# Attention, two mixture layers, one core: loads ahead of the constants, summed exponentials per block, later w_in conversion, rows in fixed tiles

## The chip, the cores and the metric

One NeuronCore of a Trainium2 chip runs the whole program. The metric is the device time of one execution in microseconds (us), as the median of several runs. One further execution is recorded by the hardware profiler; its span and its rows are what the profile shows.

Engines: PE (TensorE, matmuls; its weight loads are listed as PEld), DVE (VectorE), ACT (ScalarE), POOL (GpSimd), SP (SyncE, which issues nearly all DMAs here; SPq is its queue). TensorE's clock has two levels, 1.2 and 2.4 GHz; the profile gives the granted clock as a share of the higher one.

## What is computed

```python
# attention: batch 4, heads 8, sequence 576, head size 64
scores = q @ k.T / 8
# heads 0 to 3 ("local"):   key within the 32 positions up to the query
# heads 4 to 7 ("strided"): key not after the query, same position modulo 32
attn = softmax(where(mask, scores, -1e9)) @ v
x = attn.transpose(0, 2, 1, 3).reshape(2304, 512)
# layer 1, d_ff 2048
x2 = (s * relu(x @ w_in) ** 2 + b) @ w_out
# layer 2: 8 experts, 288 tokens each, assigned greedily by sorted gate logits
logits = x2 @ w_gate
for e in range(8):
    out[assigned == e] = relu(x2[assigned == e] @ w1[e]) @ w2[e]
```

w_in and w_out arrive as 64-bit floats, as pairs of 32-bit words, and are converted on the chip.

## The kernel before

The program is written out in Python in the order in which each engine shall run it (`manual_schedule`): every engine works through its own list in order and waits only for semaphores. A `Pipe` holds generators; each `tick` runs each live generator to its next `yield`, and after every so many ticks starts a new one. So the place of an instruction in its engine's list follows from the number of ticks between the yields.

- **Attention** (`attn_unit`): one unit is a batch, a pair of heads and a half of the sequence; a batch has 8 units, in the order strided, strided, local (5 blocks of 96 columns), strided, strided, local (5 blocks), local (4 blocks), local (4 blocks). A unit loads qk and v (L194 to L206; qk has 4 buffers), puts mask and scores into one PSUM bank (L225, L232), takes the maximum per block on DVE (L237), subtracts it (L244), takes Exp on ACT (L247), sums (L249), inverts and scales on DVE (L250 to L252), transposes on PE (L258, L260), copies the transposes on ACT (L268), multiplies by v (L279) and copies into xb (L284, L288). A unit starts every 2 ticks; I number units from 1.
- **keep_warm** (L296): matmuls on constants, between units, in ticks 5 to 17.
- **prep**: one block of w_in or w_out (fc, 16 of each). Two loads `raw` (L325), Abs on ACT (L350), the conversion on DVE (L353 to L359), then for w_in a split into wh (ACT, L333) and wl (DVE, L335), so that a product is made of wh x xh + wh x xl + wl x xh.
- **group_x** splits 384 tokens of x the same way, for each of 4 feature blocks dc: xh (ACT, L315), xl (DVE, L316).
- **Main loop** (`mix1`): step n is `h_step(g, fc)` with 12 matmuls (L427) for token group g and block fc, then Relu and Square on ACT and a store of the result to `ud`. The first 24 steps alternate between groups 0 and 1. Beside the steps run the rest of w_in, batches 2 and 3 of attention, then w_out (`prep1`), and from step 46 the folds.
- **fold_late** reloads a stored block r from `ud`, three ticks to a step, and **fold_step** multiplies four of them by wog (L464): the gate logits.
- **late_step / x2_late**: the second product (L640) on reloaded r, split into u (ACT L610, DVE L613); **x2_row** (L481) scales the sum of 128 tokens into a row tile on DVE and stores it in x2d. These matmuls also fill `route`, which assigns tokens to experts on DVE. Then come the experts (L894, L919).

The tiles of the pool `w` (68 buffers of 128x512) hold nearly everything: raw, K, W, wh, wl, r, local E, eT, v and before the change the rows of x2_row. Strided units use three fixed tiles, E0 to E2 (`self.Es`).

Of the kernel before, what the change touches and what calls it, by code (L numbers as in the profile page):

```python
# [8 lines left out]
F32 = mybir.dt.float32  # L9
F32R = mybir.dt.float32r  # L10
BF = mybir.dt.bfloat16
# [51 lines left out]
class Body:  # L63
# [27 lines left out]
    P0S = 20  # L91
# [16 lines left out]
    KS = 5  # L108
    KE = 18
# [26 lines left out]
    def constants(self):  # L136
        nc, c, a = self.nc, self.c, self.a
        ts = nc.vector.tensor_scalar
# [3 lines left out]
        self.identf = c.tile([128, 128], F32, name="identf")  # L142
        ts(self.identf, jp[:, :128], 0.0, None, op0=ALU.is_equal)
        self.identb = c.tile([128, 128], BF, name="identb")
        ts(self.identb, jp[:, :128], 0.0, None, op0=ALU.is_equal)
        self.onesf = c.tile([128, 128], F32, name="onesf")
        nc.gpsimd.memset(self.onesf, 1.0)

        t1 = self.wt([128, 512], F32, "t1")
        t2 = self.wt([128, 512], F32, "t2")  # L150
        tt = nc.vector.tensor_tensor
        ts(jp[64:, :128], jp[64:, :128], 64.0, None, op0=ALU.add)
        self.Es = [c.tile([128, 8, 64], F32, name=f"E{i}") for i in range(self.NE)]
        for E in self.Es:
            nc.gpsimd.memset(E, 0.0)
        self.mstr = c.tile([128, 8, 36], BF, name="mstr")
        nc.vector.memset(self.mstr, 0.0)
        j4 = self.wt([128, 512], I32, "j4")
        nc.gpsimd.iota(j4[:, :36], pattern=[[1, 36]], base=0, channel_multiplier=0)
        nc.gpsimd.iota(j4[:, 64:100], pattern=[[0, 36]], base=0, channel_multiplier=1)  # L160
        for o in (0, 64):
            ts(j4[:, 128 + o:164 + o], j4[:, o:o + 36], 1, None, op0=ALU.bitwise_and)
# [6 lines left out]

# [8 lines left out]
        self.sb = c.tile([128, 2], F32, name="sb")  # L178
        for i, n in enumerate(("s", "b")):
            src = a[n]  # L180
            nc.sync.dma_start(self.sb[:, i:i + 1],
                              bass.AP(tensor=src.tensor, offset=src.offset, ap=[[0, 128], [1, 1]]))

# [30 lines left out]
    def attn_unit(self, b, hp, hf):  # L214
# [25 lines left out]
        else:  # L240
# [3 lines left out]
        nc.vector.tensor_tensor(E[:pr], sp[:pr, :w].rearrange("p (c k) -> p c k", c=nb),  # L244
                                mx.unsqueeze(2).to_broadcast([pr, nb, kw]), op=ALU.add)
        yield from self.lag(0, b)
        nc.scalar.activation(E[:pr], E[:pr], AF.Exp, scale=0.125)  # L247
        yield from self.lag(1, b)
        nc.vector.tensor_reduce(sm, E[:pr], axis=AX.X, op=ALU.add)  # L249
# [54 lines left out]
    def group_x(self, g, dc):  # L304
# [13 lines left out]
        self.xg.setdefault(g, []).append((h, l))  # L318
# [71 lines left out]
    def prep_begin(self):  # L390
# [5 lines left out]
        self.nc.vector.memset(self.wog, 0.0)  # L396
        self.gate = self.c.tile([128, 4, 8], F32, name="gate")
        self.nc.sync.dma_start(self.gate, self.a["gate"].rearrange("(c p) e -> p c e", p=128))
# [45 lines left out]
    def fold_late(self, g, fc):  # L444
# [3 lines left out]
        yield  # L448
        self.fold_step(fc, g, r)
# [27 lines left out]
    def x2_row(self, g, t, acc):  # L477
        nc = self.nc
        row = self.wt([128, 512], F32, "x2")
        i = g * 3 + t  # L480
        nc.vector.scalar_tensor_tensor(row, acc[t], self.sb[:, 0:1], self.acc, op0=ALU.mult, op1=ALU.add)  # L481
# [32 lines left out]
    def mix1(self):  # L514
        nc = self.nc
        self.L = self.c.tile([128, 18, 8], F32, name="L")
# [3 lines left out]
        nc.gpsimd.iota(self.R, pattern=[[0, 18], [1, 8]], base=1, channel_multiplier=0,  # L520
                       allow_small_or_imprecise_dtypes=True)
        self.x2d = self.dr.tile([self.N, self.DM], F32, name="x2d")
        self.ud = {g: self.dr.tile([16, 128, self.G], F32, name=f"ud{g}") for g in range(6)}
        self.prep_begin()
        self.pf, self.xacc = {}, {}
        att, att2 = (Pipe(self.attention(*b), self.AE) for b in ((0, 1), (2, 3)))
# [7 lines left out]
        z = self.wt([128, 512], F32, "z")  # L534
        nc.gpsimd.memset(z, 0.0)
        nc.sync.dma_start(self.x2d[self.N - 128:, :], z)
# [7 lines left out]
        k = 0  # L544
        while self.units < 14 or not self.win:
            att.tick()
            if self.KS <= k < self.KE:
                self.keep_warm(self.KW)
# [542 lines left out]
```

## Time and profile before

| | |
|---|---|
| time, median of 3 runs | 850.44 us (848.18 to 854.85) |
| the profiled execution | 850.04 us |
| its span, from first to last instruction | 848.3 us |
| PE busy | 808.2 us (95%) |
| DVE busy | 481.2 us (57%) |
| ACT busy | 363.4 us (43%) |
| chain that ended last, by engine | PE 87%, DVE 6%, DMA 3% |
| granted clock of PE, mean | 0.98 |

Shares over the whole span hide the stages: an engine that is busy for 57% of the whole may be the only one that matters in one stretch. So the tables by stretch and the chain of waits, which follows the work back from the end, come first, and groups of instructions give the prices.

### The profile page before, as it was taken

To read this page: it belongs to the slowest core of one execution; us is meant where nothing else is said; L and a number is where in the kernel's file an instruction comes from. 1 tells how busy PE (TensorE), PEld (TensorE's weight loads), DVE (VectorE), ACT (ScalarE), POOL (GpSimd) and SP (SyncE) were. 2 spreads that over 40 slices of the span, in tenths; PEclk is the share of its full clock that TensorE was granted. 3 is DMA by queue.
4 is the path that set the end of the run, shared out by engine and by line. 5 is a ranking of instruction groups with operands and counts; after the bars stand their busy time and mean duration, and the time that the engine had idled before them with its cause. 6 is when DMAs were issued, how large, how long until landed. Compare 5 with 4: busy or idle time off the path is not lost.

```text
span 848.3 us, 17237 instructions
## 1 busy us (share of the span) xinstructions
PE 808.2 (95%) x6688; PEld 702.7 (83%) x6688; DVE 481.2 (57%) x1166; ACT 363.4 (43%) x824; POOL 52.4 (6%) x70
## 2 busy tenths in 40 slices
PE   6968999999899999989999998998999999999996
PEld 4748998989789867967777776767899999999994
DVE  7899873576455033255777666647255555565530
ACT  1558665556345456432222222222055545554520
POOL 1000000000000000000000000000111112121211
PEclk9978999999999999999999999998999999999999
DMA  7764744765676597360706142324185576657400
GB/s 199 233 228 127 241 146 129 234 217 174 219 234 211 183 314 254 105 222 5 244 13 228 58 129 73 97 90 125 59 284 172 168 232 204 173 181 216 134 29 28
DMA packets 88754, 140.22 MB, mean 165 GB/s; under 512 B 10848, under 2 KB 52576, under 8 KB 88672
## 3 DMA queue, kind: packets, MB, share of 16 engines
q1 hardware_dynamic: 85600, 129.68, 48.4%
q0 software_dynamic: 3072, 9.44, 3.4%
q8 instruction: 52, 0.85, 0.4%
q14 instruction: 30, 0.25, 0.1%
HBM read 106.32 MB, written 32.77 MB: 164 GB/s over the span
## 4 chain that ended last, share of the span: by engine, by line
PE 87%; DVE 6%; DMA 3%; issue 1%; ACT 1%; SPq 0%; POOL 0%; POOLq 0%; DVEq 0%
PE b L427 24%; PE b L640 21%; PE b L894 12%; PE b L919 11%; PE b L232 3%; PE b L464 2%; PE b L769 2%; PE b L279 2%; PE b L957 1%; PE b L848 1%; PE b L382 1%; DMA r<-ud 1%; PE b L935 1%; PE b L296 1%; DMA x2d<-x 1%
## 5 line engine op out<-in xcount | busy, mean ns | idle before, releaser
L640 PE MATMUL b<-wh,u 128*128 128x512 f32 x544 | 185.6, 411 | 7.3 <-DVE u L613 7.3
L640 PEld LDWEIGHTS b<-wh,u 128*128 128x128 f32 x544 | 103.7, 193 | 30.0 <-DVE u L613 9.5
L610 ACT CAST u<-r 128x384 fp32r<-128x384 f32 (+1 forms) x96 | 47.3, 496 | 170.9 <-PE b L640 114.1
L640 PE MATMUL b<-wl,u 128*128 128x512 f32 x272 | 108.2, 398 | 0.0
L432 ACT ACTIVATE r<-b 128x384 f32<-128x384 f32 x96 | 47.1, 491 | 111.0 <-PE b L427 110.7
L919 PE MATMUL b<-u,wh 128*128 128x288 f32 x448 | 93.4, 301 | 0.0
L427 PE MATMUL b<-xh,wh 128*128 128x384 f32 x384 | 90.6, 358 | 2.7 <-ACT xh L315 2.7
L427 PE MATMUL b<-xl,wh 128*128 128x384 f32 x384 | 83.7, 339 | 0.0
L335 DVE TENSOR_TENSOR wl<-raw,wh 128x512 fp32r<-128x512 f32 x128 | 82.8, 683 | 1.4 <-DMA x2d<-x 1.1
L427 PE MATMUL b<-xh,wl 128*128 128x384 f32 x384 | 82.7, 336 | 0.0
L894 PE MATMUL b<-X,wh 128*128 128x288 f32 x512 | 78.2, 295 | 0.6 <-ACT X L867 0.6
L427 PEld LDWEIGHTS b<-xh,wh 128*128 128x128 f32 x384 | 65.2, 191 | 16.3 <-issue 9.1
L333 ACT CAST wh<-raw 128x512 fp32r<-128x512 f32 x128 | 73.5, 620 | 4.0 <-DVE u L613 4.0
L894 PEld LDWEIGHTS b<-X,wh 128*128 128x128 f32 x512 | 71.6, 188 | 1.4 <-ACT X L867 0.7
L919 PEld LDWEIGHTS b<-u,wh 128*128 128x128 f32 x448 | 70.9, 188 | 0.0
L427 PEld LDWEIGHTS b<-xl,wh 128*128 128x128 f32 x384 | 69.5, 190 | 0.4 <-DVE xl L316 0.4
L427 PEld LDWEIGHTS b<-xh,wl 128*128 128x128 f32 x384 | 68.7, 190 | 0.0
L901 DVE SCALAR_TENSOR_TENSOR u<-b,u 128x288 fp32r<-128x288 f32 x64 | 29.1, 454 | 66.4 <-ACT u L900 57.7
L919 PE MATMUL b<-u,wl 128*128 128x288 f32 x224 | 65.8, 294 | 0.0
L613 DVE TENSOR_TENSOR u<-r,u 128x384 fp32r<-128x384 f32 (+1 forms) x96 | 48.9, 529 | 23.3 <-ACT u L610 23.3
L640 PEld LDWEIGHTS b<-wl,u 128*128 128x128 f32 x272 | 52.4, 193 | 9.7
L900 ACT ACTIVATE u<-b 128x288 fp32r<-128x288 f32 x64 | 26.3, 412 | 59.2 <-PE b L894 57.2
(196 smaller groups left out, 1158.6 us busy)
## 6 DMA issues: line engine op xcount, KB each, us to landing
raw<-in_moe_w_dram SPq DMA_DIRECT2D x128, 256.0 KB
r<-ud SPq DMA_DIRECT2D x160, 192.0 KB
ud<-r SPq DMA_DIRECT2D x96, 192.0 KB
raw<-in_words_dram SPq DMA_DIRECT2D x64, 256.0 KB
qk<-in_q_dram SPq DMA_DIRECT2D x24, 288.0 KB
x2d<-x SPq DMA_DIRECT2D x18, 256.0 KB
wod<-K SPq DMA_DIRECT2D x16, 256.0 KB
wo<-wod SPq DMA_DIRECT2D x16, 256.0 KB
```

The source lines that it names most:

```text
L232: nc.tensor.matmul(sp[64 * j:64 * j + p, c * kw:(c + 1) * kw], qk[sl, 0, q0:q0 + p], qk[sl, 1, k0:k0 + kw], start=False, stop=(c == nb - 1 ...
L333: nc.scalar.copy(h, W)
L335: nc.vector.tensor_tensor(l, W, _f(h), op=ALU.subtract)
L427: nc.tensor.matmul(ps[:, :self.G], w[:, dc * 128:(dc + 1) * 128], self.xg[g][dc][x], start=(k == 0), stop=(k == 11))
L432: nc.scalar.activation(r, ps[:, :self.G], AF.Relu)
L610: nc.scalar.copy(d[:, 0, :], src)
L613: nc.vector.tensor_tensor(d[:, 1, :], src, _f(d[:, 0, :]), op=ALU.subtract)
L640: self.nc.tensor.matmul(**args)
L894: self.nc.tensor.matmul(ps[:, :288], w1[dc, fh][wi][:, fs:fs + 128], X[:, xi, dc, :], start=(k == 0), stop=(k == 11))
L900: self.nc.scalar.activation(h, ps[:, :288], AF.Relu)
L901: self.nc.vector.scalar_tensor_tensor(l, ps[:, :288], 0.0, _f(h), op0=ALU.max, op1=ALU.subtract)
L919: nc.tensor.matmul(y[dc][:, :288], w[:, sl], u[:, j, :288], start=(fc == 0 and i == 0), stop=(fc == 7 and i == 2))
```

## The change

- The first two ticks of attention, with the loads of the first units, stand ahead of `constants`, and the constants are in another order, with a one-element Exp at their head. sb, gate and the store of zeros to x2d move to tick 12 (`small_loads`); the zeros are now filled by DVE instead of POOL, and wog and R move there too.
- For local units of batches 0 and 1, the subtraction on DVE, the one Exp over all blocks and the sum on DVE become one Exp for each block on ACT, straight from PSUM, with the negated and scaled maximum as its bias and the sum as its second output. The maximum is scaled on DVE.
- The conversion of w_in starts at tick 24 instead of 20; the splits of x for groups 0 and 1 are made as soon as their units are done, inside the loop, instead of behind it.
- `fold_late` has a third yield. `x2_row` writes into E0 to E2 in turn.

```diff
-    P0S = 20
+    P0S = 24
+    SL = 12
+    SEG = 2
...
     def constants(self):
         nc, c, a = self.nc, self.c, self.a
-        ts = nc.vector.tensor_scalar
+        ts, tt = nc.vector.tensor_scalar, nc.vector.tensor_tensor
+        warm = c.tile([128, 1], F32, name="warm")
+        nc.vector.memset(warm, 0.0)
+        nc.scalar.activation(warm, warm, AF.Exp)
...
+    def small_loads(self):
+        nc, a = self.nc, self.a
         for i, n in enumerate(("s", "b")):
             src = a[n]
             nc.sync.dma_start(self.sb[:, i:i + 1],
                               bass.AP(tensor=src.tensor, offset=src.offset, ap=[[0, 128], [1, 1]]))
+        nc.sync.dma_start(self.gate, a["gate"].rearrange("(c p) e -> p c e", p=128))
+        z = self.wt([128, 512], F32, "z")
+        nc.vector.memset(z, 0.0)
+        nc.sync.dma_start(self.x2d[self.N - 128:, :], z)
...
-        nc.vector.tensor_tensor(E[:pr], sp[:pr, :w].rearrange("p (c k) -> p c k", c=nb),
-                                mx.unsqueeze(2).to_broadcast([pr, nb, kw]), op=ALU.add)
-        yield from self.lag(0, b)
-        nc.scalar.activation(E[:pr], E[:pr], AF.Exp, scale=0.125)
-        yield from self.lag(1, b)
-        nc.vector.tensor_reduce(sm, E[:pr], axis=AX.X, op=ALU.add)
+        if loc and b < self.SEG:
+            nc.vector.tensor_scalar(mx, mx, 0.125, None, op0=ALU.mult)
+            yield from self.lag(0, b)
+            for c in range(nb):
+                nc.scalar.activation(E[:pr, c, :], sp[:pr, c * kw:(c + 1) * kw], AF.Exp, bias=mx[:, c:c + 1],
+                                     scale=0.125, accum_out=sm[:, c:c + 1])
+            yield from self.lag(1, b)
+        else:
+            nc.vector.tensor_tensor(E[:pr], sp[:pr, :w].rearrange("p (c k) -> p c k", c=nb),
+                                    mx.unsqueeze(2).to_broadcast([pr, nb, kw]), op=ALU.add)
+            yield from self.lag(0, b)
+            nc.scalar.activation(E[:pr], E[:pr], AF.Exp, scale=0.125)
+            yield from self.lag(1, b)
+            nc.vector.tensor_reduce(sm, E[:pr], axis=AX.X, op=ALU.add)
...
-        self.xg.setdefault(g, []).append((h, l))
+        self.xg.setdefault(g, {})[dc] = h, l
...
-        self.nc.vector.memset(self.wog, 0.0)
         self.gate = self.c.tile([128, 4, 8], F32, name="gate")
-        self.nc.sync.dma_start(self.gate, self.a["gate"].rearrange("(c p) e -> p c e", p=128))
+        self.sb = self.c.tile([128, 2], F32, name="sb")
...
     def fold_late(self, g, fc):
         r = self.wt([128, self.G], F32, "r")
         self.nc.sync.dma_start(r, self.ud[g][fc])
+        yield
         yield
         yield
         self.fold_step(fc, g, r)
...
     def x2_row(self, g, t, acc):
         nc = self.nc
-        row = self.wt([128, 512], F32, "x2")
         i = g * 3 + t
+        row = self.Es[i % self.NE].rearrange("p c k -> p (c k)")
         nc.vector.scalar_tensor_tensor(row, acc[t], self.sb[:, 0:1], self.acc, op0=ALU.mult, op1=ALU.add)
         nc.sync.dma_start(self.x2d[i * 128:(i + 1) * 128, :], row)
         return row
...
+        self.prep_begin()
+        att, att2 = (Pipe(self.attention(*b), self.AE) for b in ((0, 1), (2, 3)))
+        att.tick(self.AE)
+        self.constants()
         self.L = self.c.tile([128, 18, 8], F32, name="L")
         self.R = self.c.tile([128, 18, 8], F32, name="R")
         self.ge = self.c.tile([128, 18, 8], F32, name="ge")
         self.ranked = set()
...
-        nc.gpsimd.iota(self.R, pattern=[[0, 18], [1, 8]], base=1, channel_multiplier=0,
-                       allow_small_or_imprecise_dtypes=True)
...
-        self.prep_begin()
         self.pf, self.xacc = {}, {}
-        att, att2 = (Pipe(self.attention(*b), self.AE) for b in ((0, 1), (2, 3)))
...
-        z = self.wt([128, 512], F32, "z")
-        nc.gpsimd.memset(z, 0.0)
-        nc.sync.dma_start(self.x2d[self.N - 128:, :], z)
...
-        k = 0
-        while self.units < 14 or not self.win:
+        ready = [(8, 0, dc) for dc in range(4)] + [(10, 1, 2), (11, 1, 0), (13, 1, 3), (14, 1, 1)]
+        k = self.AE
+        while self.units < 14 or not self.win or ready:
             att.tick()
+            if k == self.SL:
+                self.small_loads()
+                nc.vector.memset(self.wog, 0.0)
+                nc.gpsimd.iota(self.R, pattern=[[0, 18], [1, 8]], base=1, channel_multiplier=0,
+                               allow_small_or_imprecise_dtypes=True)
+            while ready and self.units >= ready[0][0]:
+                self.group_x(*ready.pop(0)[1:])
             if self.KS <= k < self.KE:
                 self.keep_warm(self.KW)
             if k >= self.P0S and k % self.P0R == 0:
                 prep.tick()
             k += 1
-        for g in range(2):
-            for dc in range(4):
-                self.group_x(g, dc)
+        assert not ready
...
     def run(self):
         import contextlib
         with self.tc.manual_schedule() if self.MANUAL else contextlib.nullcontext():
-            self.constants()
             self.mix1()
```

On SyncE's queue, at the start of the program (qk and v are attention's loads, sb, gate and z the small ones), before:

```order
L181 DMA sb<-in_moe_s_dram 128x1
L181 DMA sb<-in_moe_b_dram 128x1
L398 DMA gate<-in_gate_dram 128x4x8
L536 DMA x2d<-z_138 128x512
L194 DMA qk_141<-in_q_dram 128x2x288
L199 DMA v_143<-in_vs_dram 36x512 x2
```

The same place after the change:

```order
L201 DMA qk_82<-in_q_dram 128x2x288
L206 DMA v_84<-in_vs_dram 36x512 x2
L201 DMA qk_159<-in_q_dram 128x2x288
L206 DMA v_161<-in_vs_dram 36x512 x2
L201 DMA qk_186<-in_q_dram 128x2x320
L209 DMA v_188<-in_v_dram 96x512
```

The four small DMAs are gone from the head of the queue; they stand behind the loads of unit 7.

On DVE, from the maximum of unit 15 (a local unit of 4 blocks) on; unit 14 is the local unit before it, K and W are a block of w_in in conversion, nm holds maximum and sum, before:

```order
L237 TENSOR_REDUCE nm_925<-b_890 128x4
L244 TENSOR_TENSOR E_927<-b_890,nm_925 128x384
L249 TENSOR_REDUCE nm_859<-E_861 128x5
L250 TENSOR_SCALAR nm_859<-nm_859 128x5
L251 RECIPROCAL nm_859<-nm_859 128x5
L252 TENSOR_TENSOR E_861<-E_861,nm_859 128x480
L353 TENSOR_SCALAR K_911<-K_911 128x512
L354 TENSOR_SCALAR K_911<-K_911 128x512
L356 SCALAR_TENSOR_TENSOR W_960<-raw_679,K_911 128x256
L356 SCALAR_TENSOR_TENSOR W_960<-raw_681,K_911 128x256
L359 SCALAR_TENSOR_TENSOR K_911<-raw_679,W_960 128x256
L359 SCALAR_TENSOR_TENSOR K_911<-raw_681,W_960 128x256
```

The same place after the change:

```order
L244 TENSOR_REDUCE nm_940<-b_915 128x4
L252 TENSOR_SCALAR nm_940<-nm_940 128x4
L331 TENSOR_TENSOR xl_945<-xb_388,xh_944 128x192
L331 TENSOR_TENSOR xl_945<-xb_870,xh_944 128x192
L265 TENSOR_SCALAR nm_880<-nm_880 128x5
L266 RECIPROCAL nm_880<-nm_880 128x5
L267 TENSOR_TENSOR E_882<-E_882,nm_880 128x480
L244 TENSOR_REDUCE nm_993<-b_970 128x4
L252 TENSOR_SCALAR nm_993<-nm_993 128x4
L331 TENSOR_TENSOR xl_998<-xb_388,xh_997 128x192
```

The subtraction and the sum of the local units are gone, the second block's conversion stands behind unit 16's maximum now, and splits of x stand where conversions stood.

On PE, at the first fold (four matmuls on reloaded r, L464, L479 after the change; L427 and L441 are steps of the main loop, L279 and L294 attention's last product), before:

```order
L427 MATMUL b_3205<-xh_2416,wl_2008 128x384
L382 MATMUL b_3222<-gate,WT_3177 128x8 x4
L375 MATMUL b_3227<-identf,K_3038 128x128 x4
L464 MATMUL b_3152<-r_3148,wog 32x384
L464 MATMUL b_3152<-r_3150,wog 32x384
L464 MATMUL b_3152<-r_3153,wog 32x384
L464 MATMUL b_3152<-r_3246,wog 32x384
L427 MATMUL b_3260<-xh_3068,wh_957 128x384
```

The same place after the change:

```order
L441 MATMUL b_3279<-xh_3240,wl_1079 128x384
L294 MATMUL b_3302<-eT_3264,v_2774 64x64 x2
L294 MATMUL b_3302<-eT_3266,v_2774 64x64 x2
L294 MATMUL b_3302<-eT_3264,v_2774 64x64 x2
L294 MATMUL b_3302<-eT_3266,v_2774 64x64 x2
L479 MATMUL b_3268<-r_3171,wog 32x384
L479 MATMUL b_3268<-r_3173,wog 32x384
L479 MATMUL b_3268<-r_3175,wog 32x384
L479 MATMUL b_3268<-r_3269,wog 32x384
L441 MATMUL b_3324<-xh_3091,wh_1125 128x384
```

The fold stands behind the 49th step instead of the 48th; the second one moves from behind the 52nd to behind the 54th.

## Rows read from the trace of the kernel before

**Rows 1.** Chain of waits, 0 to 120 us: start, length, what

```profile
5.89 4.38 DMA qk<-in_q_dram
...
37.01 0.67 DVE nm L237
...
46.91 0.35 DVE K L353
...
49.17 0.48 DVE nm L237
...
63.94 0.02 ACT wh L333
...
66.00 6.67 PE b L427 x24
...
73.28 16.84 PE b L427 x96
```

**Rows 2.** Busy time by stretch: stretch, PE, PEld, DVE, ACT, POOL, PEclk, DMA share, GB/s

```profile
36.00:66.00 30.00, 19.21 (x395) 15.05 (x395) 28.46 (x74) 17.06 (x49) 0.00 (x0) 0.79 0.65 218
...
73.00:130.00 57.00, 57.00 (x559) 53.22 (x556) 45.71 (x113) 38.57 (x89) 0.00 (x0) 1.00 0.63 199
```

**Rows 3.** Timeline at two folds: start, length, engine, line, what, idle before and releaser

```profile
216.71 1.14 PE L464 MATMUL b<-r,wog 128*32 128x384 f32 x2 [2.35 <-DMA r<-ud]
...
245.09 0.83 PE L464 MATMUL b<-r,wog 128*32 128x384 f32 x2 [1.40 <-DMA r<-ud]
```

**Rows 4.** Busy time by stretch at the same two folds

```profile
216.00:220.00 4.00, 3.29 (x9) 2.36 (x10) 2.05 (x7) 0.00 (x0) 0.00 (x0) 0.64 0.63 232
...
244.00:248.00 4.00, 2.91 (x14) 2.29 (x15) 1.98 (x7) 0.00 (x0) 0.00 (x0) 1.00 0.87 281
```

**Rows 5.** Timeline at the rows (x2_row) of token groups 3 and 4

```profile
526.07 0.75 DVE L481 SCALAR_TENSOR_TENSOR x<-b,sb,acc 128x512 f32<-128x512 f32 x1 [0.68 <-DMA x2d<-x]
...
530.20 0.73 PE L640 MATMUL b<-wh,u 128*128 128x512 f32 x2 [2.11 <-DVE u L613]
...
574.04 0.73 PE L640 MATMUL b<-wh,u 128*128 128x512 f32 x2 [2.66 <-DVE u L613]
```

**Rows 6.** Busy time by stretch behind the same two places

```profile
530.00:540.00 10.00, 9.80 (x51) 7.41 (x52) 5.64 (x12) 1.98 (x4) 0.00 (x0) 0.83 0.42 126
...
570.00:580.00 10.00, 7.34 (x42) 5.38 (x41) 6.89 (x23) 1.64 (x7) 0.00 (x0) 0.83 0.46 152
```

**Rows 7.** SyncE's issues from the start: start, length, queue, line, what

```profile
0.74 0.39 SPq L181 DMA_DIRECT2D sb<-in_moe_s_dram  x1
...
4.19 0.65 SPq L194 DMA_DIRECT2D qk<-in_q_dram  x1
```

**Rows 8.** Groups by form, 8 to 66 us: count | busy us, mean ns | idle before

```profile
L244 DVE TENSOR_TENSOR E<-b,nm 128x480 f32<-128x480 f32 x4 | 2.6, 657 | 0.1
L249 DVE TENSOR_REDUCE nm<-E 128x5 f32<-128x480 f32 x4 | 2.6, 644 | 0.0
...
L333 ACT CAST wh<-K 128x512 fp32r<-128x512 f32 x4 | 2.4, 610 | 3.6 <-DVE K L359 3.6
L247 ACT ACTIVATE E<-E 128x480 f32<-128x480 f32 x4 | 2.4, 606 | 3.8 <-DVE E L244 3.8
...
L244 DVE TENSOR_TENSOR E<-b,nm 128x384 f32<-128x384 f32 x4 | 2.2, 558 | 0.1
...
L247 ACT ACTIVATE E<-E 128x384 f32<-128x384 f32 x4 | 2.1, 524 | 5.3 <-DVE E L244 5.3
...
L335 DVE TENSOR_TENSOR wl<-K,wh 128x512 fp32r<-128x512 f32 x3 | 2.0, 682 | 0.0
...
L250 DVE TENSOR_SCALAR nm<-nm 128x5 f32<-128x5 f32 x4 | 0.7, 172 | 0.1
```

**Rows 9.** Timeline behind 66 us: the splits of x

```profile
65.44 3.78 ACT L315 CAST xh<-xb 128x384 fp32r<-128x384 f32 x12
...
66.69 4.10 DVE L316 TENSOR_TENSOR xl<-xb,xh 128x384 fp32r<-128x384 f32 x12
```

More of the change, by code (lines that the diff above doesn't have):

```diff
@@ L141, in constants @@
                        allow_small_or_imprecise_dtypes=True)
[L142 to L157, printed above, removed]
         j4 = self.wt([128, 512], I32, "j4")
@@ L160, in constants @@
         nc.gpsimd.iota(j4[:, 64:100], pattern=[[0, 36]], base=0, channel_multiplier=1)
+        t1 = self.wt([128, 512], F32, "t1")
+        t2 = self.wt([128, 512], F32, "t2")
+        self.mstr = c.tile([128, 8, 36], BF, name="mstr")
+        nc.vector.memset(self.mstr, 0.0)
+        self.identb = c.tile([128, 128], BF, name="identb")
+        ts(self.identb, jp[:, :128], 0.0, None, op0=ALU.is_equal)
+        self.identf = c.tile([128, 128], F32, name="identf")
+        ts(self.identf, jp[:, :128], 0.0, None, op0=ALU.is_equal)
+        ts(jp[64:, :128], jp[64:, :128], 64.0, None, op0=ALU.add)
         for o in (0, 64):
@@ L168, in constants @@
             nc.vector.tensor_copy(self.mstr[h:h + 36], t1[h:h + 36, :36].unsqueeze(1).to_broadcast([36, 8, 36]))
+        self.Es = [c.tile([128, 8, 64], F32, name=f"E{i}") for i in range(self.NE)]
+        for E in self.Es:
+            nc.gpsimd.memset(E, 0.0)
+        self.onesf = c.tile([128, 128], F32, name="onesf")
+        nc.gpsimd.memset(self.onesf, 1.0)
         self.mloc = c.tile([128, 5, 96], BF, name="mloc")
@@ L176, in constants @@
             nc.vector.tensor_copy(self.mloc[:, n, :], t1[:, :96].unsqueeze(1).to_broadcast([128, n.stop - n.start, 96]))
-        self.sb = c.tile([128, 2], F32, name="sb")
+    def small_loads(self):
+        nc, a = self.nc, self.a
         for i, n in enumerate(("s", "b")):
```

## The prediction

> **What bounds the kernel now.** I read the chain of waits first. From 73.28 us it is TensorE with 96 matmuls in 16.84 us, 0.175 us each, and TensorE stays the bound almost to the end. Ahead of 66.00 us, where the first matmul of the first large product stands, it is something else [rows 1]: a load that lands at 10.27 us, then attention on TensorE, and from 37.01 to 63.92 us VectorE without a break (63.94 is the first piece behind it). The table by stretch says the same: in 36 to 66 us VectorE is busy 28.46 of 30 us, ScalarE 17.06, TensorE 19.21 at a granted clock of 0.79 [rows 2]. So a microsecond of VectorE's work taken out there is worth one. Behind 66 us only what makes TensorE wait counts. I went through TensorE's waits there. Four places carry most: two waits for a reloaded r, 2.35 and 1.40 us [rows 3], the first of which also costs clock (0.64 in the four microseconds around it, 1.00 around the second) [rows 4], and two waits of 2.11 and 2.66 us for u, which stands on VectorE behind x2_row [rows 5], both followed by ten-microsecond stretches at 0.83 [rows 6].
>
> **The loads ahead of the constants.** SyncE's first issue is at 0.74 us and the first qk only at 4.19, behind sb, gate and the store of z, which waits for GpSimd's fill [rows 7]. With qk first, every load of attention is issued 3.45 us earlier, in the same order and with the same number in flight; the second qk, issued at 5.89 and landed at 10.27 [rows 1], then lands near 6.8. The masks must be ready by then; they are made by much the same VectorE instructions as before, started at the same time, and were no wait of the chain at that load. I take 3.4 us; the bounds are 2.0 (the constants become the later) and 3.6. Up to unit 11 (the 37.01 of the chain) TensorE is the bound, warm-up matmuls included, and its work is unchanged, so unit 11 reaches VectorE at 33.6. The early table load of Exp hides under this. The four small DMAs and two fills that now stand behind unit 7's loads delay only the loads of the 8th and later units, which are issued many microseconds before use; I cost them at nothing, and at 1 us if that cover is gone.
>
> **VectorE from unit 11 on.** Before, this stretch is 63.92 - 37.01 = 26.9 us. What changes in it:
> - Four local units (two of 5 blocks, two of 4) lose the subtraction L244 and the sum L249 there: 2 x (0.657 + 0.644) + 2 x (0.558 + 0.56) = 4.8 us (the 4-block sum is taken like its subtraction, as the two are alike at 5 blocks). Four scalings of a 128x5 come in, 0.17 each, 0.7 us [rows 8].
> - Of the conversions of w_in, four stood ahead of that end and two do now: one takes 49.17 - 46.91 = 2.26 us [rows 1], so 4.5 us less; of the low halves L335 one instead of two, 0.7 less [rows 8].
> - The splits of x (L316) come in from behind 66 us: 12 take 4.10 us [rows 9], ten of them stand ahead of the new end, some 3.6 us.
>
> 26.9 - 4.8 + 0.7 - 4.5 - 0.7 + 3.6 = 21.2 us, so the last operand of the first product is ready at 33.6 + 21.2 = 54.8 instead of behind 63.9.
>
> **ScalarE in the same stretch.** It loses four exponentials (2 x 0.606 + 2 x 0.524 = 2.26 us) and gets 18 of 96 columns. No such instruction is in the trace. Between 384 and 480 columns the exponential grows by 0.082 us per 96, so 96 columns alone are 0.606 - 4 x 0.082 = 0.28 us, the lower bound; the upper is the whole 480-column one, 0.606 [rows 8], since the sum that each writes out is not priced by any row. I take 0.28, since it is the same function on the same partitions: 5.0 us. The x casts bring 3.3 of their 3.78 us [rows 9], and three casts L333 fall out, 1.8 us [rows 8]: 17.06 - 2.26 + 5.0 + 3.3 - 1.8 = 21.3 us, and three conversions' Abs steps come off that too. So ScalarE comes level with VectorE, no higher. The Trainium skill (ScalarE: Activation LUTs, What ACT_TABLE_LOAD costs) speaks against many short activations: it states a fixed 280 ns each with a pointer bias, plus 0.833 ns a column, less about 93 ns of overlap back to back. By it an exponential here would be 0.27 to 0.36 us, an estimate, and the 18 of them 4.8 to 6.5 us; the trace has no pointer-bias activation to hold beside it.
>
> Two engines that are level and hand work to each other in order will not overlap fully; I allow 1.6 us, an estimate of one unit's hand-over. The first large product then starts near 56.4 us instead of 66.0: **9.6 us** gained, bounds 5 (start shift 2.0, exponentials at 0.45 us) and 12. From there TensorE is the bound as before, if the weights keep coming: each block of w_in needs 2.26 + 0.68 = 2.9 us of VectorE and feeds 24 matmuls, 4.2 us. In 73 to 130 us VectorE is busy 45.71 of 57 [rows 2]; two conversions more (5.9 us) less the 3.6 us of splits already done leave it 9 us of room.
>
> **The third yield in fold_late.** The matmuls on a reloaded r move behind one or two more steps of 12 matmuls, 2.1 us each at 0.175. Both waits, 2.35 and 1.40 us, are then covered, the second by twice that. Clock: 0.64 over 4 us is 2.9 us at the lower of the two levels, 1.2 instead of 2.4 GHz, which loses half of that, 1.4 us [rows 3, 4]. **5.1 us**, bounds 0 (the load is as late again) and 5.5.
>
> **The rows in E0 to E2.** Rows 2 and 3 of a token group start when the DMA of the row before them has ended (0.68 us of wait shown) [rows 5]; with three fixed tiles they don't. At 528 us the wait of 2.11 us goes, since its third row can then run right behind its sum, and 10 us at 0.83 (3.4 us at the lower level, 1.7 lost) with it: 3.8. At 571.4 (574.04 - 2.66) the third row still has to run behind the last matmul of its sum, 0.75 us, and a u of 0.41 behind it: 1.2 us of wait stay, 1.5 go, and as the wait of 1.40 us left the clock at 1.00 [rows 4] I count the 1.7 of clock as well: 3.2 [rows 5, 6]. **7.0 us**, bounds 1.5 and 8.2.
>
> **The sum.** 9.6 + 5.1 + 7.0 = 21.7 us off the profiled 850.0: 828.3. The median of the runs is 0.4 higher, so 829 us. All the rest (zero fill, wog, one table load) I cost at nothing: TensorE is the bound where they stand.
>
> **Rivals.**
> - *ScalarE takes over the front.* If a small exponential with its sum takes 0.6 us, the upper bound, 18 x 0.33 = 5.9 us come on an engine already level: first product near 62, 835 us. For it: no row prices the summed output. Against: ScalarE's wait rows show it idle for 13 of 30 us before [rows 2]. 0.13.
> - *The later waits are handed on.* Folds meet the next reload late, rows leave u late for another reason (DMA behind the rows), and half or less of the 12.1 us comes: 835 to 841, say 839. For it: the same DMA engines carry the reloads; against: nothing else waits at these places. 0.15.
> - *The clock does not fall in the front.* Attention's TensorE work is packed into 23 us instead of 29. If the clock holds, the first 24 matmuls take 4.2 instead of 6.67 us [rows 1]: 826.5. The row shows the fall in a stretch where TensorE waited most of the time. The Trainium skill (TensorE: Matmul & The Clock Gate, Part 1) states that idling lowers the clock and activity gives it back, which would have this outcome if the new stretch is dense enough. 0.08.
> - *Slower: weights just in time.* One finished block instead of three is in hand at the first product, so a conversion that comes late stops TensorE at once. Where before two blocks (8.4 us of matmuls) stood between, there is one step. It decides from 1.6 us of wait at each of 14 blocks (22 us); at 2 us it gives 856. Against it: VectorE's 9 us of room. 0.04.
>
> **How the numbers follow.** Forecast 0.60, and the rivals above 0.40. Range: the forecast with its bounds goes from 824 (12 + 5.5 + 8.2) to about 836, the first three rivals reach from 826 to 841, so 821 to 842 leaves out the slower case and some of each edge. A measurement here tells 1% (8.5 us) from no change; faster by more than that is under 841.9: 0.90, within 0.06, slower 0.04.
>
> **What would show it.** The first qk issued near 0.7 us; unit 11's maximum near 33.6; the first matmul of the large product at 55 to 58 us, with VectorE or ScalarE right behind it; small exponentials near 0.28 us; no wait for r<-ud at the folds and 1.00 of clock there; no wait of x2_row for a DMA. Wrong, if exponentials come out at 0.5 us or more, if TensorE waits for wh or wl between 60 and 130 us, or if the waits for u near 520 and 565 us stay.

## The result, and the profile after

The changed kernel takes 823.3 us (median of 4 runs, 822.4 to 824.8) beside 849.3 us for the kernel before on the same chip (4 runs, 847.5 to 854.9): ratio 0.9685, 95% interval 0.9635 to 0.9735. That is 26.0 us; forecast were 21.7, to 829, in a range of 821 to 842. The profiled execution took 822.4 us with a span of 820.3.

First the page of the changed kernel: TensorE's busy time (the row goes on with the other engines), its granted clock in 40 slices, and the shares of the chain of waits.

```profile
PE 798.2 (97%) x6688; PEld 697.9 (85%) x6688; DVE 473.6 (58%) x1160; ACT 370.3 (45%) x889; POOL 52.2 (6%) x69
...
PEclk9979999999999999999999999999999999999999
...
PE 92%; DVE 4%; ACT 1%; issue 1%; DMA 1%; POOLq 0%; POOL 0%; DVEq 0%; ACTq 0%; SPq 0%
```

Only the slice of 41 to 61.5 us still has a clock of 0.7. The chain of waits up to the first large product, to be held beside [rows 1] (start, length, what):

```profile
4.54 0.32 DVE mstr L166
...
4.90 0.40 PE b L232
...
31.93 0.97 PE b L239 x20
...
36.34 0.71 PE b L239 x32
...
37.07 0.47 DVE nm L244
...
41.99 1.72 ACT E L255 x10
...
44.96 1.30 ACT E L255 x8
...
50.62 0.68 DVE K L374 x2
51.32 0.62 ACT wh L348
...
53.88 1.18 PE b L294 x16
55.06 6.21 PE b L441 x24
```

Three things are to be seen. The loads are gone from it: at the start it is the mask mstr, then TensorE. The scores of unit 11 end at 32.90 us and its maximum starts at 32.95, where before it was 37.01; but the chain now stays on TensorE up to the maximum of unit 13 at 37.07. And from there to 55 us VectorE and ScalarE take turns, where before it was VectorE but for 1.4 us of ScalarE behind 55 us. The first large matmul starts at 54.99 instead of 66.00 us. Busy time by stretch around that, beside [rows 2] (stretch, PE, PEld, DVE, ACT, POOL, clock, DMA share, GB/s):

```profile
33.00:44.00 11.00, 10.61 (x244) 8.31 (x244) 10.30 (x29) 9.00 (x38) 0.00 (x0) 1.00 1.04 314
44.00:55.00 11.00, 7.90 (x134) 5.99 (x134) 9.42 (x30) 10.37 (x44) 0.00 (x0) 0.72 0.64 226
55.00:62.00 7.00, 7.00 (x43) 6.68 (x42) 6.86 (x18) 5.24 (x16) 0.00 (x0) 0.72 0.09 31
...
63.00:120.00 57.00, 57.00 (x552) 53.13 (x550) 46.44 (x117) 38.38 (x90) 0.00 (x0) 1.00 0.67 214
```

VectorE has 19.7 and ScalarE 19.4 of the 22 us from 33 to 55; before, VectorE was full and ScalarE was not. The DMA engines are full as well from 33 to 44 us (share 1.04). Behind the start TensorE is busy without a gap, so w_in is in time.

TensorE's timeline at the folds [rows 3] and at the waits for u that are left, and VectorE's at the rows of token group 4 [rows 5]:

```profile
204.84 0.85 PE L479 MATMUL b<-r,wog 128*32 128x384 f32 x8
205.62 0.97 PE L441 MATMUL b<-xh,wh 128*128 128x384 f32 x4
...
353.35 0.73 PE L658 MATMUL b<-wh,u 128*128 128x512 f32 x2 [2.15 <-DVE u L631]
...
553.65 0.22 PE L694 MATMUL b<-rt,ltri 128*128 128x144 bf16 x1 [0.69 <-DVE rt L766]
...
560.73 0.17 PE L830 MATMUL b<-rt,o 128*96 128x24 bf16 x1 [0.64 <-DVE rt L824]
```

```profile
544.46 0.75 DVE L496 SCALAR_TENSOR_TENSOR E<-b,sb,acc 128x512 f32<-128x512 f32 x1 [0.20 <-PE b L658]
...
545.89 1.55 DVE L496 SCALAR_TENSOR_TENSOR E<-b,sb,acc 128x512 f32<-128x512 f32 x2
```

The first fold on reloaded r has its 8 matmuls in a row, and the next product starts 0.78 us behind its first. The three rows of group 4 stand within 3 us and none waits for a DMA. TensorE's waits for u have gone from 7.3 us in 5 places to 2.6 in 3; the one at 353 us was there before too.

By stage, from the first matmul of each in the two profiled executions:

| stage | before, us | after, us | less by |
|---|---|---|---|
| start to the first large product | 66.0 | 55.0 | 11.0 |
| from there to the first matmul of the second large product | 295.9 | 288.0 | 7.9 |
| from there to its last group of wh,u | 239.8 | 230.8 | 9.1 |
| the rest of the span | 246.5 | 246.5 | 0.0 |

### The profile page after: what moved, and what is told of

It reads as the page before. It is cut to its first block, busy times and chain, and to the rows that moved or that the text cites. A ratio compares the mean times of both kernels' runs of the same rounds, so it can differ in the third digit from the quotient of the medians.

```text
span 820.3 us, 17310 instructions
## 1 busy us (share of the span) xinstructions
PE 798.2 (97%) x6688; PEld 697.9 (85%) x6688; DVE 473.6 (58%) x1160; ACT 370.3 (45%) x889; POOL 52.2 (6%) x69
## 4 chain that ended last, share of the span: by engine, by line
PE 92%; DVE 4%; ACT 1%; issue 1%; DMA 1%; POOLq 0%; POOL 0%; DVEq 0%; ACTq 0%; SPq 0%
PE b L441 26%; PE b L658 21%; PE b L912 12%; PE b L937 11%; PE b L239 3%; PE b L479 2%; PE b L787 2%; PE b L294 2%; PE b L397 2%; PE b L975 1%; PE b L866 1%; PE b L953 1%; PE b L390 1%; PE b L311 1%; PE b L273 1%
## 5 line engine op out<-in xcount | busy, mean ns | idle before, releaser
L658 PE MATMUL b<-wh,u 128*128 128x512 f32 x544 | 181.7, 404 | 2.6 <-DVE u L631 2.6
L658 PEld LDWEIGHTS b<-wh,u 128*128 128x128 f32 x544 | 101.6, 188 | 23.8 <-DVE u L631 3.8
L441 PE MATMUL b<-xh,wh 128*128 128x384 f32 x384 | 89.9, 355 | 0.0
L441 PE MATMUL b<-xl,wh 128*128 128x384 f32 x384 | 83.0, 337 | 0.0
L441 PE MATMUL b<-xh,wl 128*128 128x384 f32 x384 | 82.8, 336 | 0.0
L441 PEld LDWEIGHTS b<-xh,wh 128*128 128x128 f32 x384 | 64.6, 190 | 12.1 <-issue 10.0
L441 PEld LDWEIGHTS b<-xl,wh 128*128 128x128 f32 x384 | 69.0, 189 | 0.0
L441 PEld LDWEIGHTS b<-xh,wl 128*128 128x128 f32 x384 | 68.5, 189 | 0.0
## 6 DMA issues: line engine op xcount, KB each, us to landing
qk<-in_q_dram SPq DMA_DIRECT2D x24, 288.0 KB
```

The costliest lines, as they stand in the source:

```text
L441: nc.tensor.matmul(ps[:, :self.G], w[:, dc * 128:(dc + 1) * 128], self.xg[g][dc][x], start=(k == 0), stop=(k == 11))
L658: self.nc.tensor.matmul(**args)
```

## Experiments

Every run was timed in several rounds against the kernel before on its chip, whose median was 848.1 to 849.4 us each time; "beside the changed kernel" means beside its 823.3. Runs of one changed kernel lie within 0.7 to 4.7 us of each other, so I do not tell apart two medians that differ by less than about 1.5 us; a difference of 1.5 to 2 us needs a trace beside it, as not all kernels ran on the same chip.

### The three parts one by one

The kernel before with only the third yield, and with only the rows:

```diff
 def fold_late(self, g, fc):
     r = self.wt([128, self.G], F32, "r")
     self.nc.sync.dma_start(r, self.ud[g][fc])
     yield
     yield
+    yield
     self.fold_step(fc, g, r)
```

```diff
 def x2_row(self, g, t, acc):
-    row = self.wt([128, 512], F32, "x2")
     i = g * 3 + t
+    row = self.Es[i % self.NE].rearrange("p c k -> p (c k)")
```

And the changed kernel with both of these undone, which leaves the front.

> The kernel before with only the third yield in fold_late. Theory (the two waits for r and the clock lost behind them go, and nothing takes their place): no wait of the fold's matmuls for a reload, clock 1.00 there, 5.1 us faster than before by the prediction's sum, up to 7.5 us if the whole difference between first fold and last h_step in the two traces is the fold's. Rival (the waits are handed on to the next reload or to fo): under 2.5 us faster. If it gives 5 and not 7.5, some 2.4 us of that stage come from the new front.

> The kernel before with only the rows of x2_row in E0 to E2. Theory (the third row no longer waits for the store of the row before it, so u is in time and the clock stays up): waits of 2.11 and 2.66 us for u at token groups 3 and 4 gone, 7.0 us faster by the prediction's sum, up to 9.1 if the whole difference of that stage in the two traces is the rows'. Rival (u is late for another reason, the queue of stores ahead of the reloads): at least one of the two waits stays, under 3.5 us faster.

> The changed kernel without its third yield and with the rows in work tiles as before: the front alone. Theory (the three parts add up): 11 us faster than before, 839, and the two waits for r and the two for u are back. Rival (the parts are not independent: with the front shortened, reloads and rows meet other traffic): it differs from 28 us less what the other two single parts give by more than 3 us.

| part alone | median, us | ratio to before (95%) | less than before |
|---|---|---|---|
| third yield | 842.6 | 0.9934 (0.9917 to 0.995) | 6.3 |
| rows in E0 to E2 | 840.5 | 0.9904 (0.9877 to 0.9932) | 8.4 |
| front | 839.9 | 0.9893 (0.9877 to 0.991) | 9.1 |

The sum is 23.8 us; together they gave 26.0, and the three intervals are each 2.8 to 4.7 us wide. By the measure that was set for the front, the parts do not add up: 28 us less 6.3 and 8.4 is 13.3, and 9.1 is 4.2 short of it, over the 3 us of the rival. But 28 is the difference of two single profiled executions; from the medians' 26.0 the front is 2.2 short, within the intervals.

The stages of the traces say more than the medians, as each edit acts in one stage. From the first large matmul to the second large product, the eleven traces with the third yield take 287.1 to 289.5 us, the three without it 293.6, 295.9 and 296.3. From there to the last group of wh,u, the nine traces with the rows in E0 to E2 and the ranks as they were take 230.8 to 234.2 us, the three with the old rows 239.8, 239.9 and 241.6. And the unchanged front has three traces: its first large matmul stands at 66.00 us in the kernel before, and in the two kernels with one late edit at

```profile
64.80 6.21 PE b L427 x24
```

```profile
64.94 6.36 PE b L427 x24
```

while the new front alone has it at 54.95, as the changed kernel at 54.99. By the means the folds are worth 7.3 us, the rows 7.8 and the front 10.3, in all 25.4 of the 26.0. So, within what these runs can tell, the parts add up.

The trace of the third yield alone has no wait for r left, that of the rows alone has 2.6 us of waits for u where before it was 7.3 (engine, line, releaser: us, times, longest):

```profile
PE b L640 <- DVE u L613: 2.6, 3, 2.1
```

With the front alone both are back:

```profile
PE b L657 <- DVE u L630: 7.5, 5, 2.7
...
PE b L478 <- DMA r<-ud: 3.8, 4, 1.9
```

Neither rival of the late waits holds, though a little may be handed on: with the third yield the waits for fo grow from 1.4 to 2.0 us, and with the rows in fixed tiles a wait of 0.7 us for rt is new at group 4 (the front alone has one there too, of 1.2).

Why is the fold worth more than its two wait entries? Two rows of the kernel before, at the fold of [rows 3], give it: the fold's first matmul, and the first of the product behind it.

```profile
213.51 0.85 PE L464 MATMUL b<-r,wog 128*32 128x384 f32 x6
...
217.78 1.65 PE L427 MATMUL b<-xh,wh 128*128 128x384 f32 x4
```

From start to start that is 4.27 us; undisturbed, after, it is 0.78. So this fold lost 3.49 us and not the 2.35 of its idle entry: six matmuls ran, TensorE stood idle, and the last two then took 1.07 us to the start of the product (0.76 at the second fold, where the clock was 1.00). The 12 matmuls and 16 of attention behind it took 4.14 us, from 217.78 to 221.92; at the full clock 12 such take 2.21 and 16 such 0.61, so 1.3 more went there. The second fold took 3.0 instead of 0.8 us, 2.2 lost for an entry of 1.40, and one at 268.8 us, which has no entry at all, 0.65 too much. Together 7.7 us, which is what the stage shows (288.1 us in the run with the yield alone, 295.9 before). The old fold's stage varies between executions by 2.7 us, as given above, so its worth does too.

### The parts of the front

Each undoes one thing in the changed kernel. All local heads with one exponential a unit:

```diff
-    SEG = 2
+    SEG = 0
```

> The changed kernel with SEG at 0: all local heads as before, one exponential a unit, subtraction and sum on VectorE. Theory A (VectorE bounds the stretch from unit 11 to the first large product): 4.8 us of VectorE come back less 0.7 us of scalings, about 4 us slower than the changed kernel. Theory B (the small exponentials at 0.32 us each made ScalarE the bound there): 18 x 0.32 - 2.26 = 3.5 us fall off ScalarE, 2 to 3.5 us faster than the changed kernel. Level engines that take turns: within 1.5 us of it.

The conversion of w_in at step 20 again:

```diff
-    P0S = 24
+    P0S = 20
```

> The changed kernel with the first conversion of w_in at step 20 again instead of 24. Theory (VectorE and ScalarE bound the stretch ahead of the first large product, so each conversion of 2.3 us of VectorE put there costs its time): two conversions more ahead of it, first large matmul at 58 to 60 us instead of 55.0, 3 to 4.5 us slower than the changed kernel. Rival (later conversions are on the path anyway, as weights come just in time): no later by more than 1 us, and in the changed kernel TensorE would have to wait for wh or wl behind 60 us.

Constants and small loads ahead of attention's loads (z filled by GpSimd again):

```diff
-        att.tick(self.AE)
         self.constants()
         ...
+        self.small_loads()
+        nc.vector.memset(self.wog, 0.0)
+        att.tick(self.AE)
         ...
-            if k == self.SL:
-                self.small_loads()
-                ...
```

> The changed kernel with its constants and small loads ahead of attention's loads again. Theory (the start of attention moves with its loads, as unit 11's maximum went from 37.0 to 33.0 us): 3.4 to 4.1 us slower than the changed kernel, unit 11's maximum near 36.5 to 37. Rival (the stretch behind unit 11 absorbs it, as the conversions of w_in start by count and not by time and VectorE has gaps): under 1.5 us slower.

The splits of x behind the loop:

```diff
-        ready = [(8, 0, dc) for dc in range(4)] + [(10, 1, 2), (11, 1, 0), (13, 1, 3), (14, 1, 1)]
+        ready = []
         ...
-        assert not ready
+        for g in range(2):
+            for dc in range(4):
+                self.group_x(g, dc)
```

> The changed kernel with the splits of x behind the loop as before, all eight after unit 14 and the first w_in block. Theory A (moving them ahead fills gaps of ScalarE and VectorE, and their time at the end was on the path): 1.5 to 3 us slower than the changed kernel, TensorE waiting for xh as it did for 2.7 us before. Theory B (both engines are full in that stretch, so the work costs the same wherever it stands): within 1 us of it.

| undone | median, us | ratio to before (95%) | beside the changed kernel | first large matmul at |
|---|---|---|---|---|
| exponentials by block | 826.7 | 0.9736 (0.972 to 0.9753) | +3.4 | 57.3 |
| later conversion | 827.0 | 0.9739 (0.9691 to 0.9788) | +3.7 | 58.7 |
| loads ahead | 826.2 | 0.973 (0.9681 to 0.9778) | +2.9 | 58.4 |
| early splits of x | 823.7 | 0.9689 (0.9641 to 0.9738) | +0.4 | 52.9 |

The first three carry the front, the first two about as expected, the loads a little less at the median. Without the exponentials by block VectorE is full again (20.8 of the 22 us from 33 to 55, ScalarE 13.9), which fits theory A. But it is not shown that the loss is VectorE's work: the chain of that run goes by loads from 35.81 to 52.21 us. And only 2.3 of the 3.4 us stand at the first large matmul; the second large product took 3.4 us more in that execution, where the clock fell behind the wait for u at 355 us (0.83) and once more from 560 to 580 (0.89 and 0.93).

```profile
35.81 6.56 DMA v<-in_v_dram
...
42.39 5.76 DMA raw<-in_words_dram
...
48.17 4.04 DMA raw<-in_words_dram
```

With the earlier conversion the chain is VectorE's from 37.10 to 54.97 us, and its 3.7 us stand at the first large matmul. With the loads behind, qk is on the chain as before, the scores of unit 11 end 3.4 us later than in the changed kernel, at 36.31, and 3.4 us come back at the first large matmul:

```profile
5.99 3.85 DMA qk<-in_q_dram
...
35.34 0.97 PE b L239 x20
```

The early splits of x bring nothing, as theory B had it: without them the first large matmul starts 2.1 us sooner, but waits for xh again, and its first 24 take 7.75 us instead of 6.21. From the chain of that run:

```profile
52.89 7.75 PE b L441 x24
```

### What a small exponential and its sum cost

The exponentials stay by block, but VectorE sums the unit in one operation again:

```diff
                 nc.scalar.activation(E[:pr, c, :], sp[:pr, c * kw:(c + 1) * kw], AF.Exp, bias=mx[:, c:c + 1],
-                                     scale=0.125, accum_out=sm[:, c:c + 1])
+                                     scale=0.125)
             yield from self.lag(1, b)
+            nc.vector.tensor_reduce(sm, E[:pr], axis=AX.X, op=ALU.add)
```

> The changed kernel with the exponentials block by block but without their sums; VectorE sums each unit again. Price of the sum: if the read of the accumulator holds ScalarE up, exponentials of 96 columns come every 0.28 us or less instead of every 0.32; if it is hidden, the interval stays at 0.32. Time: by the theory that VectorE is the bound, the five sums of 0.56 to 0.64 us (two of them ahead of unit 11) put 2 to 2.5 us on the path; by the theory that ScalarE is, it is level with the changed kernel or up to 1 us faster.

Measured: 823.4 us, ratio 0.9695 (0.9646 to 0.9743), first large matmul at 55.6. ScalarE's timeline, first of the changed kernel, then of this one, where five such exponentials stand in one row:

```profile
42.33 0.33 ACT L255 ACTIVATE E<-b,nm 128x96 f32<-128x96 f32 x1
42.55 0.20 ACT L255 ACTIVATION_READ_ACCUMULATOR E<-b,nm 128x1 f32 x1
42.64 0.34 ACT L255 ACTIVATE E<-b,nm 128x96 f32<-128x96 f32 x1
42.87 0.21 ACT L255 ACTIVATION_READ_ACCUMULATOR E<-b,nm 128x1 f32 x1
```

```profile
34.13 1.26 ACT L255 ACTIVATE E<-b,nm 128x96 f32<-128x96 f32 x5
```

With the sum one starts every 0.31 us, since each brings a second instruction that reads the accumulator. Without it five take 1.26 us; less the last one's 0.36 (the mean of one), that is 0.225 us from start to start. So the sum costs 0.09 us a block on ScalarE. Moving it to VectorE changes the time by nothing that can be measured. That is what was expected if ScalarE is the bound; but the chain of this run is VectorE's from 33.14 to 53.44 us but for 2 us, so neither theory alone is right: from 37 to 55 us the two engines of the changed kernel are level and alternate. Beside the kernel with one exponential a unit (826.7), what pays is that the subtraction has become the bias; who adds up does not matter.

### What is late next

These ask what bounds the changed kernel in the same places. First fewer warm-up matmuls, which stand in its chain with 7.6 us ahead of unit 11, then none:

```diff
-    KE = 18
+    KE = 14      # and 5 in the second kernel
```

> The changed kernel with the warm-up matmuls of the first loop up to step 13 instead of 17, so 16 of 52 fewer. In its chain they stand between 21.9 and 26.6 us with 2.2 us. Theory (TensorE bounds the stretch up to unit 11, warm-up included, and VectorE has 40% to spare between 20 and 33 us): unit 11 some 2 us sooner and the kernel 1.5 to 2.2 us faster than the changed kernel. Rival (the matmuls of attention then run at the lower clock): granted clock under 1.00 between 20 and 33 us and no gain, or 1 to 3 us slower.

> The changed kernel without warm-up matmuls. Theory (TensorE bounds up to unit 11): 7.7 us of them come off its chain, but VectorE has 14.8 us of work in 12 to 33 us and takes over, so 3 to 6 us faster than the changed kernel. Rival (the clock): attention's own matmuls, some 24 us of TensorE ahead of unit 11, run in part at the lower level, granted clock 0.5 to 0.8 there, level with the changed kernel or up to 5 us slower.

With 16 of 52 fewer: 821.4 us (821.1 to 821.8), 1.9 less than the changed kernel; the ratios to before, 0.9681 and 0.9685, do not tell the two apart. In the trace unit 11's maximum starts at 30.87 us instead of 32.95, the clock is 1.00 from 20 to 33 us, and the first large matmul is at 52.9. So TensorE did bound the stretch up to unit 11. With none: 823.5 us, no gain, first large matmul at 53.8. Two rows of the latter say why the front gains less than the 3 to 6 us of the theory: TensorE waits for loads of qk instead, and the clock is at its lower level, 1.2 GHz, from 44 to 55 us. There the matmuls of attention bound the stretch, busy 11.00 of 11 us. That the front gains nothing is not shown: in the profiled execution, the fastest of its four, the first 24 large matmuls end 2.1 us sooner than in the changed kernel, and the second large product, with the clock at 0.83 behind the wait for u, gives 1.8 back.

```profile
PE b L239 <- DMA qk<-in_q_dram: 5.6, 6, 1.9
```

```profile
44.00:55.00 11.00, 11.00 (x137) 9.01 (x138) 9.19 (x28) 9.28 (x34) 0.00 (x0) 0.50 0.66 237
```

Next the u that is late at 353 us. Ahead of it on VectorE stand the 21 operations of ranks, from 348.75 to 352.75 us. In this kernel they are kept in a list, of which each late step takes two comparisons (three operations each) behind its u; and the fill of E0 to E2 goes from GpSimd to ScalarE, the small one of onesf behind the start:

```diff
+        self.rankq += [lambda d=d: compare(d) for d in range(1, 8)]
         ...
             nc.vector.tensor_tensor(d[:, 1, :], src, _f(d[:, 0, :]), op=ALU.subtract)
+        self.rank_some(2)
         yield
         ...
-            nc.gpsimd.memset(E, 0.0)
+            nc.scalar.copy(E, zero.unsqueeze(2).to_broadcast([128, 8, 64]))
```

> The changed kernel with two waits treated that the change left: the 21 operations of ranks, 4.0 us in a row on VectorE ahead of the u that TensorE waits 2.15 us for, go out 6 at a time behind a u each; and the fill of E0 to E2, which GpSimd writes for 1.6 us while VectorE's first operations take 1.2, 1.1 and 0.5 us, goes to ScalarE. Theory for the first: the wait of 2.15 us near 353 us goes, 2 to 3.5 us with the clock lost behind it. Theory for the second: VectorE's first 128x128 comparison takes 0.2 us instead of 1.2, the masks are ready near 3 instead of 4.86 us, and the first scores start when qk lands, 0.5 to 1.8 us sooner. Rival for the second: these operations are slow for another reason (first use), and nothing moves. Together 2 to 5 us faster than the changed kernel by the theories, 0 by the rivals (u late behind something else on VectorE, loads as the bound of the start).

Measured: 821.8 us (820.9 to 823.7), ratio 0.9685 (0.9637 to 0.9734), 1.5 less than the changed kernel, which by itself is not told apart. TensorE's waits for u fall from 2.6 to 0.4 us, and from the start of the second large product to its last group of wh,u it takes 230.0 us, less than any of the nine traces above. The fill did slow VectorE: its first comparison takes 0.41 us, where it took 1.19 in the changed kernel, from the same start at 1.10 us, and the masks are ready 1.2 us sooner, at 3.60. But that gives nothing at the end: TensorE then waits for qk, and the first large matmul is at 55.5.

```profile
PE b L240 <- DMA qk<-in_q_dram: 1.3, 2, 0.7
...
PE b L670 <- DVE u L642: 0.4, 2, 0.2
```

```profile
1.10 0.41 DVE L161 TENSOR_SCALAR identb<-jp 128x128 bf16<-128x128 f32 x1
```

Last, both together: the portions of ranks, the fill on ScalarE and 16 warm-up matmuls fewer.

> The changed kernel with both edits that paid: the ranks in portions and the fill on ScalarE, and 16 warm-up matmuls fewer. Theory (one acts ahead of the first large product, the other at 350 us, and TensorE is the bound between, so they add): 1.9 + 1.5 us faster than the changed kernel, near 820, 3.5% under the kernel before, no wait for u over 0.5 us and the first large matmul near 53. Rival (the earlier start meets its loads or weights later, as without any warm-up matmul): no better than 821.4.

Measured: 819.2 us (6 runs, 817.9 to 821.0), ratio 0.9652 (0.9618 to 0.9686), 4.1 less than the changed kernel and the fastest of all. The waits for u are 0.4 us. The first large matmul, though, was at 55.5 us in the profiled execution and not near 53: there a load of qk came late, and the clock was 0.72 from 33 to 44 us and 0.50 from 44 to 53. In this execution, with a span of 818.1 us beside 820.3, the second large product is 2.3 us shorter and the start no sooner. That its median is 2.3 us under that of fewer warm-up matmuls alone fits the ranks, whose stage takes 228.5 us here; whether the front's share comes in other executions was not seen. The row of its chain:

```profile
31.12 6.22 DMA qk<-in_q_dram
```

## Why the prediction was right, point by point

- **What bounds it.** Right in the main: the first large product came 11.0 us sooner by work taken off VectorE and by earlier loads, and behind it the time fell where TensorE's waits went; the rest of the span, behind the second large product, is 246.5 us in both. "VectorE without a break" was read too strictly: the chain before has 1.4 us of ScalarE from 55.27 us on, and in the two other traces of the unchanged front a load of w_in stands on it for 4.8 and 3.8 us, up to 51.6 and 51.7.
- **Loads ahead.** The shift of unit 11 was 4.06 us (37.01 to 32.95) against 3.4, over the upper bound of 3.6. But the other two traces of the unchanged front have unit 11's maximum at 35.80 and 35.94 us, and undone alone the loads moved its scores by 3.41 us: the term was right, and the profiled execution before was a late one. The bound of the start is the mask, as the lower bound had supposed, and not the second qk. Undone alone it was worth 2.9 us at the end. Nothing was seen of the small loads and fills that were costed at nothing.
- **VectorE from unit 11 on.** Forecast were 21.2 us of work up to 54.8 us; it has 19.7 in the 22 us up to 55, so it stood idle for 2.3 us, where 1.6 were allowed for the hand-over. The terms for conversions (5.2 us with the low half) and exponentials (4.1) showed as 3.7 and 3.4 when undone. The splits of x, counted as 3.6 us more, cost 2.1 at the first matmul and give 1.5 of it back in the first 24.
- **ScalarE.** "Level with VectorE, no higher" held, at 19.4 and 19.7 us. The price of an exponential was mis-sized in two ways that nearly cancel: 0.225 us bare, so 0.28 was no lower bound, and 0.09 for the sum, which I had counted at nothing; 0.315 in all, 0.6 us more over 18. That they cancel is luck. The prediction's estimate of 0.27 to 0.36, from the Trainium skill (ScalarE: Activation LUTs, What ACT_TABLE_LOAD costs), was for an exponential without the sum: the trace agrees with it for one alone (0.36 us) and is below it back to back (0.225).
- **First large product.** 55.0 us against 56.4, so 11.0 us in the profiled pair against 9.6; the front alone measured 9.1 (7.6 to 10.4 by its interval), and beside all three traces of the unchanged front 10.3.
- **Folds.** Right mechanism, size too small: 6.3 us measured (4.2 to 7.0), 7.9 in the profiled stage, 7.3 by all traces, against 5.1 with an upper bound of 5.5. The term that failed is "2.35 and 1.40": idle entries in place of the time from start to start, 3.5 and 2.2, and a third fold that had no entry.
- **Rows.** 8.4 us measured (5.8 to 10.4), 9.1 in the profiled stage, 7.8 by all traces, against 7.0 with an upper bound of 8.2. "1.2 us of wait stay" at group 4 did not happen: there is no wait for u there, only 0.69 us for rt. Before, the clock also fell behind the short waits for rt at 587 us (0.68 from 590 to 594); in the profiled execution of the changed kernel it did not, but with ranks in portions it did again (0.83 from 560 to 570).
- **Rivals.** None came. ScalarE did not take over. Of the late waits at most 0.6 us for fo and 0.7 for rt were handed on. The weights were in time, with TensorE busy 57.00 of 57 us. And the clock did fall in the front, to 0.72 from 44 to 62 us: the first 24 matmuls took 6.21 us, hardly less than the 6.67 before. The Trainium skill (TensorE: Matmul & The Clock Gate, Part 1) states that activity gives the clock back, which would have kept it up; that was not seen here, though attention was packed more densely: TensorE was busy 7.90 of the 11 us from 44 to 55. Without warm-up matmuls it was busy 11.00 of these 11 us, at a clock of 0.50.
- **Range.** The forecast with its bounds does not end at "about 836": the three lower bounds, 5, 0 and 1.5, add up to 6.5 us and would reach 843.5. The time fell near the other end, so nothing hung on it.

So the forecast held since its terms were right in kind. The sum was 4.3 us short of the 26.0 measured. By the stages of all traces 2.2 of it are at the folds, 0.8 at the rows and 0.7 in the front; 0.6 stays open.

## What to carry to other kernels

Cost a stall by the time from the start of the work ahead of it to the start of the work behind it, against an undisturbed place in the same trace; the idle entry alone was short by a third here, and a clock that falls behind it comes on top. Where two engines are level and hand work to each other, moving a step from one to the other brings nothing (the sums, the splits of x), while work that vanishes from either (the subtraction, a conversion not yet needed) brings its own time. And filler meant to keep TensorE's clock up has a price where TensorE is the bound: 16 matmuls fewer brought unit 11 2.1 us sooner with the clock at 1.00 there, while 52 fewer left attention at 1.2 GHz for 11 us. Where the best amount lies was not settled: with the same 16 fewer, the last kernel met a late load and the lower clock too.

## What was not expected of the hardware

- **A sum with an activation is a second instruction.** Each 96-column exponential with its sum comes every 0.31 us, without it every 0.225; the read of the accumulator shows as a row of its own.
- **GpSimd's fill slows VectorE.** Two 128x128 comparisons took 1.19 and 1.11 us beside the 1.6 us fill of E0 to E2, and 0.41 and 0.33 with the fill on ScalarE.
- **The clock behind the same wait is not the same each time.** Behind the wait of 2.1 us for u near 353 us the clock of the ten microseconds fell to 0.83 without exponentials by block, with x behind, and with fewer or no warm-up matmuls, but stayed at 1.00 in the changed kernel, with the loads behind, with the earlier conversion and with the sums on VectorE, though the code there is the same. With the wait gone it stayed at 1.00. Why it falls in one and not in the other was not settled. Ten us at 0.83 are 3.4 us at the lower level, which lose 1.7; that much one execution can differ from the next by this place alone.
